# A fused gated-attention and ReGLU kernel: step 1's loads in another order and behind other events, and all engines' orders planned anew

## Chip, core and metric

The kernel runs on one core of one Trainium2 chip. The metric is device time in microseconds for one execution. Before the change it is 193.26 us, the median of five runs (192.61 to 194.41).

A core has five engines with a queue of instructions each: PE (TensorE, matrix products), ACT (ScalarE), DVE (VectorE), POOL (GpSimd) and SP (SyncE, which only issues DMA transfers here). Each works through its own queue in order and waits on semaphores for the others. Sixteen DMA engines carry all transfers; every load of this kernel is spread over all of them and has landed when the last of the sixteen has done its part.

## What is computed

Shapes: 4 batches, 8 heads, 768 tokens, head size 48; so 3072 tokens of 384 features go into the feed-forward network, whose hidden size is 1536.

```python
f = 1.0 / (1.0 + np.exp(-f_logit))
for t in range(S):
    state = f[:, :, t, :, None] * state + np.einsum('bhd,bhe->bhde', k[:, :, t], v[:, :, t])
    y[:, :, t] = np.einsum('bhd,bhde->bhe', q[:, :, t], state)
...
x = y.transpose(0, 2, 1, 3).reshape(B * S, H * D)
gate = np.maximum(x @ w_gate, 0.0)
val = x @ w_val
return (gate * val @ w_out).astype(np.float32)
```

## The kernel before

**Steps and pairs.** The 768 tokens are cut into six steps of 128 (steps 0 to 5, `c` in the code). Each step handles four blocks of 128 tokens, in two pairs of two; "f1.0" is the load of `f_logit` for step 1, pair 0. In steps 0 and 1 (`twos`) a pair is two consecutive 128-token chunks of one batch and goes through `attention_pair`; in steps 2 to 5 it is one chunk of each of two batches and goes through `attention_front` and `attention`.

**A pair's chain.** ACT turns f into log decays (L585, L586: exponential, then logarithm, into `bneg`). PE sums them along the tokens (L594). ACT takes exponentials (L608, `expo`), and k and q are multiplied by them into `hats` (L610): on POOL or on DVE, by the set `on_dve` and, in step 0, by a rule of its own. PE transposes `hats` (L642), k's first and q's second, DVE copies the result (L650, `qkT`), PE forms the scores (L667), DVE masks them (L683; two of them go by ACT and POOL, L678 and L680, set `by_pool`), and PE makes the rows (L712, L717), which ACT copies to `xT` (L729). POOL casts v into `vpad` (L657). The state goes by L692, L564, L568 and L570.

**The feed-forward part.** For each step `ffn_hidden` makes the hidden values, 12 blocks `j` of 128: PE multiplies `xT` by `wg` and by `wv` (L922), ACT takes the ReLU (L928), DVE the product (L932, `gT`). `ffn_out` multiplies by `wo` (L965), ACT copies (L975), SP stores (L979). PE fills the times between attention pieces with this work.

**Loads.** f, k, q and v come by SP, 384 KB each (L487). The weights come by POOL's queue, three slices of each of `wg`, `wv` and `wo` (L508); they are cast from f32 to bf16 on the way. The list `first` fixes the order of the loads of steps 0 and 1 and of all weight slices; "wg0@f0.1" means that POOL issues slice 0 of `wg` only once f0.1 has landed. Loads of SP are a chain among themselves, and so are those of POOL, and what an engine has queued behind such a wait waits too. Loads of steps 2 to 5 wait for the load three places ahead of them (`flight`).

**The planner.** The order in which each engine does its operations is worked out when the program is built. `Plan.schedule` is a list scheduler with a cost for each operation: at each step it takes the operation that can start first, by priority where several can. `Plan.transfers` simulates the two queues of loads packet by packet and gives each load of `first` a landing time, and `settle` goes through scheduling and transfers eight times. `tail` is the time that is assumed between a load's last packet and its landing, for POOL's loads and for SP's after 14 us. None of these numbers is executed; they set orders alone.

**Fillers.** Up to 15 us PE has gaps, in which products of a tile of zeros (`zeros`) keep it busy: 18 of 512 columns, one that is planned (L1015) and 17 put in gaps (L1024).

Of the kernel before, what the change touches and what calls it, by code (L numbers as in the profile page):

```python
# [8 lines left out]
BF16 = mybir.dt.bfloat16  # L9
# [33 lines left out]
class Plan:  # L43
# [143 lines left out]
    def transfers(self):  # L187

        rings = {e: [op for op in self.order[e] if op.parts] for e in ("SP", "POOL")}
        todo, at = {e: [] for e in rings}, {e: 0 for e in rings}  # L190
        issue = {"SP": 0.0}
        held = {e: [] for e in rings}
        sent, owed, t, last = 0, 0, 0.0, None
        pending = None
        sp = rings["SP"]
        queue = {e: [] for e in rings}
        for op in rings["POOL"]:
            queue["POOL"].append([op, op.parts[0], op.start + op.parts[3]])
# [24 lines left out]
        while True:  # L223
            feed()
            heads = {e: queue[e][0] for e in queue if queue[e]}
            if not heads:
                break
            can = {e: h for e, h in heads.items() if h[2] <= t}
            if not can:
                times = [h[2] for h in heads.values()]  # L230
                if nxt < len(sp) and pending is None:
                    times.append(max(sp[nxt].ready, issue["SP"]))
                t = max(t + 0.01, min(times))
                continue
            e = next(iter(can)) if len(can) == 1 else ("POOL" if last == "SP" else "SP")
            h = can[e]
            t += h[0].parts[1 if len(can) == 1 else 2] / 1000.0
            last = e
            h[1] -= 1
            if e == "SP":  # L240
                sent += 1
            if h[1] == 0:
                h[0].land = t + (self.tail[0] if e == "POOL" else 0.65 if t < 14.0 else self.tail[1])
                queue[e].pop(0)

    def settle(self, banks, rounds, early):
        self.depth, self.lag, self.tail = 250, 2.4, (1.6, 2.6)
        for i in range(rounds):
            self.schedule(banks)
            if i < rounds - 1:  # L250
                self.transfers()
                for op in self.ops:
                    if op not in early:
                        op.land = op.issued = None
        return self.order
# [47 lines left out]
def bass_hgrn2_outer__then__ffn_reglu_kernel(  # L303
# [14 lines left out]
    x_way = {(c, pr): "tiled" if c < 5 else "xbar" for c in range(6) for pr in range(2)}  # L318
    s_twin = {(c, pr) for c in range(6) for pr in range(2)}
    y_twin = {(c, pr) for c in range(2, 5) for pr in range(2)}  # L320
    on_dve = {(1, 0, 0, 0), (1, 0, 0, 1), (1, 1, 0, 0), (1, 1, 0, 1)}
    act_copies, dve_q, single = set(), set(), set()
    flight = 3
    wsteps = 3
    first = ("f0.0 k0.0 q0.0 v0.0 f0.1 k0.1 v0.1 wg0@f0.1 wv0 wg1 wv1 q0.1 wg2@wv0 wv2 f1.0@wv1 k1.0 q1.0 v1.0 wo0@q1.0 wo1 "
             "k1.1 f1.1 q1.1 v1.1@f1.1 wo2").split()
    B, H, S, D = q.shape
    C = 128
    NC = S // C
# [11 lines left out]
    sb = nc.alloc_sbuf_tensor  # L341
# [40 lines left out]
    mask2 = sb("mask2", [128, 2, 2, 64], BF16)  # L382
    ident = sb("ident", [128, 128], BF16)
    ones = sb("ones", [128, 1], BF16)
    zeros = sb("zeros", [128, 512], BF16)
    banks = [nc.alloc_psum_tensor(f"ps{i}", [128, 512], F32) for i in range(8)]

    pl = Plan({"bc": 2, "bc4": 4, "tp": 2, "s": 4, "y": 2, "kv": 2, "f": 4})
    add = pl.add
    gp, ve, sc, te, sy = nc.gpsimd, nc.vector, nc.scalar, nc.tensor, nc.sync  # L390
# [13 lines left out]
    def pool_t(n):  # L404
        return dict(occ=0.1 + n * 2.2 / 1000.0, lat=0.12)
# [29 lines left out]
    for t, name, src, sname in ((upto, "upto", tri, "tri"), (below, "below", tris, "tris")):  # L435
        add("DVE", lambda t=t, src=src: ve.tensor_tensor(t[:], src[:], same.ap[:, 0:128], ALU.mult), [same, sname], [name],
            occ=0.25, prio=-19)
    add("DVE", lambda: ve.tensor_copy(pick2[:], same.ap[:, 0:128].rearrange("p (b t) -> p b t", b=2)[:, :, 0]), [same], ["pick2"],
        occ=0.1, prio=-19)
    for i, src, name in ((0, upto, "upto"), (1, below, "below"), (1, upto, "upto")):  # L440
# [3 lines left out]
            src[:, 64:128].unsqueeze(1).to_broadcast([128, len(lo), 64]), ALU.add), [name], [f"mask2_{i}{m}" for m in lo],  # L444
            prio=-9, **pool_t(64 * len(lo)))

    fill("DVE", "zeros", zeros[:], 0.0, 256, -30)
    for i in range(NB):
        fill("DVE", f"bneg{i}", bneg[:, i], 0.0, 512, -28 if i < 1 else 11 if i < 2 else 30)
    for i in range(NH):  # L450
# [558 lines left out]
    for item in pend[:-1]:  # L1009
        ffn_out(*item)  # L1010
    ffn_end(NC - 1, B - 1, [(0, 256), (256, DM)])

    WARM = 512
    warm_until = 15.0
    add("PE", lambda: te.matmul(banks[-1][:, 0:WARM], zeros[:, 0:128], zeros[:, 0:WARM]), ["zeros"], ["warm"], occ=0.2,  # L1015
        prio=-30)
    for e in pl.ENGINES:
        pl.free0[e] = 0.8
    spare = banks[-1]
    order = pl.settle([(bk, warm_until if bk is spare else 0.0) for bk in banks], rounds=8, early=set(firsts))  # L1020
    waits = pl.needs()

    def warm():
        return te.matmul(spare[:, 0:WARM], zeros[:, 0:128], zeros[:, 0:WARM], start=True, stop=True, skip_group_check=True)  # L1024

    busy, at, begun = [], pl.free0["PE"], False
    for op in order["PE"]:
        gap, each = op.start - at, 0.44 if at < 4.0 else 0.23
        if begun and op.start <= warm_until:
            for _ in range(int((0.9 if gap > 1.5 else 0.6) * gap / each)):  # L1030
                busy.append((op, warm))
        begun = True
        at = op.start + op.occ
    fillers = {}
    for op, emit in busy:
# [2 lines left out]
    for e in ("PE", "ACT", "DVE", "POOL"):  # L1038
        n = 0
# [75 lines left out]
```

## Time and profile before

| what | value |
|---|---|
| median of five runs | 193.26 us |
| the profiled execution, its time | 193.03 us |
| its span, first to last instruction | 191.3 us |
| PE busy | 181.2 us, 95% of the span |
| DVE, ACT, POOL busy | 106.4, 109.7, 75.5 us |
| DMA moved | 32.04 MB, mean 167 GB/s |
| granted TensorE clock | 1.00 |

The first table below gives busy time by stretch; the DMA share is the mean over the 16 engines (queues overlap, so that it can pass 1).

| stretch, us | PE busy, us | DVE | ACT | POOL | DMA share |
|---|---|---|---|---|---|
| 0 to 16 | 12.90 of 16.00 | 13.41 | 10.18 | 12.77 | 0.99 |
| 16 to 45 | 25.39 of 29.00 | 21.50 | 16.11 | 12.46 | 1.13 |
| 45 to 100 | 54.74 of 55.00 | 33.42 | 39.39 | 30.35 | 1.15 |
| 100 to 150 | 49.37 of 50.00 | 26.37 | 29.30 | 19.88 | 0.83 |
| 150 to 191.3 | 38.82 of 41.30 | 11.70 | 14.74 | 0.00 | 0.14 |

The loads around the change, from the issues and landings that the trace gives:

| load | issued, us | to landing | landed |
|---|---|---|---|
| wg0, wv0, wg1 | 9.54, 10.47, 11.25 | 6.3, 7.3, 8.6 | 15.8, 17.8, 19.9 |
| wv1, wg2, wv2 | 15.01, 18.03, 19.95 | 6.7, 6.6, 6.8 | 21.7, 24.6, 26.8 |
| f1.0, k1.0 | 21.74, 22.15 | 7.4, 8.1 | 29.1, 30.3 |
| q1.0, v1.0 | 22.93, 26.70 | 8.5, 5.9 | 31.5, 32.6 |
| k1.1, f1.1 | 29.11, 30.27 | 5.3, 5.3 | 34.4, 35.6 |
| q1.1, v1.1 | 31.46, 35.58 | 12.2, 10.6 | 43.6, 46.2 |
| wo0, wo1, wo2 | 31.75, 32.55, 36.45 | 8.0, 10.1, 9.4 | 39.7, 42.6, 45.9 |
| f2.0 | 35.99 | 11.7 | 47.7 |

In the profile's lines an instruction group is given with its start, its length, engine, line and tiles; a bracket at the end gives the idle time of that engine just before it and what ended it. "issue" there means that the engine waited for nothing that the profile shows. A busy PE is one with a product in its pipeline; consecutive products overlap, so lengths of groups add up to more than the time they took.

### The profile page before, as it was taken

To read this page: it belongs to the slowest core of one execution; us is meant where nothing else is said; L and a number is where in the kernel's file an instruction comes from. 1 tells how busy PE (TensorE), PEld (TensorE's weight loads), DVE (VectorE), ACT (ScalarE), POOL (GpSimd) and SP (SyncE) were. 2 spreads that over 40 slices of the span, in tenths; PEclk is the share of its full clock that TensorE was granted. 3 is DMA by queue.
4 is the path that set the end of the run, shared out by engine and by line. 5 is a ranking of instruction groups with operands and counts; after the bars stand their busy time and mean duration, and the time that the engine had idled before them with its cause. 6 is when DMAs were issued, how large, how long until landed. Compare 5 with 4: busy or idle time off the path is not lost.

```text
span 191.3 us, 5012 instructions
## 1 busy us (share of the span) xinstructions
PE 181.2 (95%) x2061; PEld 107.9 (56%) x2079; DVE 106.4 (56%) x189; ACT 109.7 (57%) x244; POOL 75.5 (39%) x109
## 2 busy tenths in 40 slices
PE   7878899789999999999999999999999999999995
PEld 2456674446686456767645564554555555544564
DVE  7799365995736765617685284635528323343300
ACT  3785459734598576584877829566533533334322
POOL 8497503743295646547365563725400000000000
DMA  5999999999999999999999998999631310011113
GB/s 154 324 261 201 159 267 225 203 218 186 246 184 223 220 174 220 238 193 250 167 225 182 191 229 175 221 210 225 150 77 41 86 41 17 24 45 41 41 51 114
DMA packets 108854, 32.04 MB, mean 167 GB/s; under 512 B 101792, under 2 KB 108832, under 8 KB 108832
## 3 DMA queue, kind: packets, MB, share of 16 engines
q1 hardware_dynamic: 104848, 28.19, 70.6%
q0 software_dynamic: 3984, 3.54, 12.1%
q8 instruction: 16, 0.26, 0.5%
q14 instruction: 6, 0.05, 0.1%
HBM read 25.95 MB, written 4.72 MB: 160 GB/s over the span
## 4 chain that ended last, share of the span: by engine, by line
PE 76%; DMA 16%; POOL 4%; issue 2%; SPq 1%; ACT 0%; POOLq 0%
PE ps L922 41%; PE ps L965 23%; DMA q_in<-in_q_dram 7%; DMA wo<-in_moe_w_out_dram 5%; DMA wv<-in_moe_w_val_dram 4%; PE ps L852 3%; PE ps L817 2%; PE ps L751 1%; PE ps L900 1%; SPq L487 1%; PE ps L945 1%; POOL hats L610 1%; POOL vpad L657 1%; POOL wg L508 1%; PE ps L712 1%
## 5 line engine op out<-in xcount | busy, mean ns | idle before, releaser
L932 DVE TENSOR_TENSOR gT<-relu,ps 128x512 bf16<-128x512 bf16 (+1 forms) x88 | 51.1, 588 | 61.0 <-PE ps L922 37.6
L928 ACT ACTIVATE relu<-ps 128x512 bf16<-128x512 f32 (+1 forms) x88 | 45.5, 521 | 28.6 <-PE ps L922 27.3
L922 PE MATMUL ps<-xT,wv 128*128 128x512 bf16 (+1 forms) x262 | 60.7, 340 | 0.8 <-DMA wv<-in_moe_w_val_dram 0.5
L922 PE MATMUL ps<-xT,wg 128*128 128x512 bf16 (+1 forms) x249 | 57.9, 338 | 0.8 <-issue 0.2
L965 PE MATMUL ps<-wo,gT 128*128 128x384 bf16 x276 | 49.1, 326 | 0.3 <-DMA wo<-in_moe_w_out_dram 0.3
L965 PEld LDWEIGHTS ps<-wo,gT 128*128 128x128 bf16 x276 | 26.2, 98 | 18.5 <-DMA wo<-in_moe_w_out_dram 0.7
L922 PEld LDWEIGHTS ps<-xT,wv 128*128 128x128 bf16 x264 | 25.0, 98 | 19.7 <-DMA wv<-in_moe_w_val_dram 0.7
L922 PEld LDWEIGHTS ps<-xT,wg 128*128 128x128 bf16 x264 | 24.7, 98 | 19.6 <-issue 1.3
L975 ACT ACTIVATE osb<-ps 128x384 f32<-128x384 f32 x23 | 11.2, 494 | 25.8 <-PE ps L965 25.8
L827 DVE TENSOR_TENSOR ptm<-ps,tri 128x512 bf16<-128x512 f32 x32 | 20.5, 684 | 5.3 <-PE ps L817 5.2
L773 POOL TENSOR_TENSOR hats<-k_in,expo 128x384 bf16<-128x384 f32 x16 | 15.8, 998 | 18.1 <-ACT expo L761 15.2
L570 POOL TENSOR_TENSOR st<-ssum,dec 128x384 bf16<-128x384 f32 x16 | 13.1, 831 | 19.4 <-DVE ssum L568 19.3
L777 POOL TENSOR_TENSOR hats<-q_in,expo 128x384 bf16<-128x384 f32 x16 | 15.7, 997 | 5.2 <-DMA q_in<-in_q_dram 5.1
L568 DVE TENSOR_TENSOR ssum<-ps,st 128x384 f32<-128x384 f32 x16 | 8.4, 552 | 3.7 <-PE ps L900 3.5
L761 ACT ACTIVATE expo<-ps 128x384 f32<-128x384 f32 x16 | 7.9, 491 | 2.8 <-PE ps L754 2.7
L683 DVE TENSOR_TENSOR ptm<-ps,mask 128x512 bf16<-128x512 f32 x14 | 8.7, 681 | 1.1 <-PE ps L667 1.0
L807 POOL CAST vpad<-v_in 128x384 bf16<-128x384 f32 x16 | 7.6, 507 | 1.1 <-DMA v_in<-in_v_dram 1.1
L763 ACT ACTIVATE expo<-ps 128x384 f32<-128x384 f32 x16 | 8.0, 500 | 0.0
L729 ACT ACTIVATE xT<-ps 128x384 bf16<-128x384 f32 x8 | 4.2, 598 | 5.5 <-PE ps L717 5.5
L742 ACT ACTIVATE f_in<-f_in 128x768 f32<-128x768 f32 x8 | 6.7, 843 | 0.8 <-DMA f_in<-in_f_logit_dram 0.8
L744 ACT ACTIVATE bneg<-f_in 128x768 bf16<-128x768 f32 x8 | 6.7, 843 | 0.1
L881 ACT ACTIVATE xT<-ps 128x384 bf16<-128x384 f32 x12 | 5.2, 486 | 2.5 <-PE ps L852 2.5
(85 smaller groups left out, 162.2 us busy)
## 6 DMA issues: line engine op xcount, KB each, us to landing
f_in<-in_f_logit_dram SPq DMA_DIRECT2D x12, 384.0 KB, 5.8
k_in<-in_k_dram SPq DMA_DIRECT2D x12, 384.0 KB, 5.5
q_in<-in_q_dram SPq DMA_DIRECT2D x12, 384.0 KB, 4.8
v_in<-in_v_dram SPq DMA_DIRECT2D x12, 384.0 KB, 5.5
out_dram<-osb SPq DMA_DIRECT2D x23, 192.0 KB, 2.6
wg<-in_moe_w_gate_dram POOLq DMA_DIRECT2D x3, 384.0 KB, 6.6
wv<-in_moe_w_val_dram POOLq DMA_DIRECT2D x3, 384.0 KB, 6.8
wo<-in_moe_w_out_dram POOLq DMA_DIRECT2D x3, 384.0 KB, 9.4
```

Source lines behind the costliest of these rows:

```text
L568: add("DVE", lambda: ve.tensor_tensor(tmp[:, :], kv.ap[:, 0:HD], s_old[:, :], ALU.add), [kv, f"S{b}_{(c + 1) % 2}"], [key], prio=P + 8, ** ...
L570: add("POOL", lambda: gp.tensor_tensor(t4(s_new), t4(tmp), rate, ALU.mult), [key] + dk, [f"S{b}_{c % 2}"], prio=P + 8, **pool_t(HD))
L683: add("DVE", lambda i=i, j=j, mask=mask: ve.tensor_tensor(ptm[ms[i]][:, j, :, :], s[i][j].ap[:, :].rearrange("p (n t) -> p n t", n=NP), ma ...
L763: add("ACT", lambda: sc.activation(ex[:, 0, :], bc.ap[:, 0:HD], AF.Exp, scale=-1.0), [bc], [f"expq{ei // 2 * 2}_{ei % 2}"], prio=P + 1, ** ...
L773: add("POOL", lambda: gp.tensor_tensor(hk, kin[:, b % 2, :, :], ex[:, 1, :].rearrange("p (h d) -> p h d", h=H), ALU.mult), in_keys("k", c, ...
L777: add(e, lambda: engine[e].tensor_tensor(hq, qin[:, b % 2, :, :], ex[:, 0, :].rearrange("p (h d) -> p h d", h=H), ALU.mult), in_keys("q", ...
L827: add("DVE", lambda mi=mi, j=j, s=s: ve.tensor_tensor(ptm[mi][:, j, :, :], s.ap[:, :].rearrange("p (n t) -> p n t", n=NP), mask, ALU.mult) ...
L922: mm = te.matmul(bank.ap[:, 0:n], wt[:, kt, j * 128:(j + 1) * 128], xT[xi][:, kt, n0:n1], start=(kt == 0), stop=(kt == NK - 1))
L928: add("ACT", lambda: sc.activation(relu[ri][:, 0:n], gate.ap[:, 0:n], AF.Relu), [gate], [f"relu{ri}"], prio=P, **act_t(n))
L932: add("DVE", lambda: ve.tensor_tensor(gT[gi][:, j, n0:n1], relu[ri][:, 0:n], val.ap[:, 0:n], ALU.mult), [val, f"relu{ri}"], [f"gT{gi}_{j}_ ...
L965: mm = te.matmul(o[b].ap[:, 0:DM], gT[gi][:, j, b * C:(b + 1) * C], wo[:, j, :], start=(j == 0), stop=(j == NJ - 1))
L975: add("ACT", lambda b=b, oi=oi: sc.activation(osb[oi][:, :], o[b].ap[:, 0:DM], AF.Copy), [o[b]], [f"osb{oi}"], prio=P, **act_t(DM))
```

## The change

- In `first`, the order on SP after step 0 goes from f1.0 k1.0 q1.0 v1.0 k1.1 f1.1 q1.1 v1.1 to f1.0 k1.0 v1.0 k1.1 f1.1 q1.0 q1.1 v1.1, and in step 0 wg0's place in the list moves. The events behind which loads are released change: f0.1 and k0.1 get f0.0, v1.0 gets wv2, q1.0 gets f1.0, v1.1 has wo0 in place of f1.1; of the weights wg2 has k0.1 in place of wv0, wo0 has k1.1 in place of q1.0, and wo2 gets f1.1.
- In the planner, `transfers` takes a list of seven times (`fetch`) at each of which its simulated queues stand still for 0.55 us (`stall`); `tail` goes from 1.6 and 2.6 us to 1.0 and 0.7.
- One more k product, that of step 1, pair 1, first of its two halves, goes from POOL to DVE (`on_dve`).
- `zeros` has 128 columns in place of 512. The planned first filler has 128 columns; the others read the tile several times over (a broadcast) and stand in the first five gaps of PE's order that are planned longer than 0.4 us: 4 of 256 columns, then 8, 3, 1 and 2 of 512.
- With all this, the orders of all engines are worked out anew, those of the later steps too.

```diff
@@ transfers
+        fetch = list(self.fetch)
...
+            if fetch and fetch[0] <= t:
+                fetch.pop(0)
+                t += self.stall
+                last = None
+                continue
             e = next(iter(can)) if len(can) == 1 else ("POOL" if last == "SP" else "SP")
...
@@ settle
-        self.depth, self.lag, self.tail = 250, 2.4, (1.6, 2.6)
+        self.depth, self.lag, self.tail = 250, 2.4, (1.0, 0.7)
+        self.stall = 0.55
+        self.fetch = [14.1, 19.8, 26.3, 40.8, 45.8, 51.4, 57.8]
...
-    on_dve = {(1, 0, 0, 0), (1, 0, 0, 1), (1, 1, 0, 0), (1, 1, 0, 1)}
+    on_dve = {(1, 0, 0, 0), (1, 0, 0, 1), (1, 1, 1, 0), (1, 1, 0, 0), (1, 1, 0, 1)}
...
-    first = ("f0.0 k0.0 q0.0 v0.0 f0.1 k0.1 v0.1 wg0@f0.1 wv0 wg1 wv1 q0.1 wg2@wv0 wv2 f1.0@wv1 k1.0 q1.0 v1.0 wo0@q1.0 wo1 "
-             "k1.1 f1.1 q1.1 v1.1@f1.1 wo2").split()
+    first = ("f0.0 k0.0 q0.0 v0.0 f0.1@f0.0 wg0@f0.1 k0.1@f0.0 v0.1 wv0 q0.1 wg1 wv1 wg2@k0.1 f1.0@wv1 wv2 k1.0 v1.0@wv2 k1.1 f1.1 "
+             "q1.0@f1.0 q1.1 wo0@k1.1 wo1 wo2@f1.1 v1.1@wo0").split()
...
-    zeros = sb("zeros", [128, 512], BF16)
+    zeros = sb("zeros", [128, 128], BF16)
...
-    fill("DVE", "zeros", zeros[:], 0.0, 256, -30)
+    fill("DVE", "zeros", zeros[:], 0.0, 64, -30)
...
-    add("PE", lambda: te.matmul(banks[-1][:, 0:WARM], zeros[:, 0:128], zeros[:, 0:WARM]), ["zeros"], ["warm"], occ=0.2,
-        prio=-30)
+    add("PE", lambda: te.matmul(banks[-1][:, 0:128], zeros[:, :], zeros[:, :]), ["zeros"], ["warm"], occ=0.1, prio=-30)
...
-    def warm():
-        return te.matmul(spare[:, 0:WARM], zeros[:, 0:128], zeros[:, 0:WARM], start=True, stop=True, skip_group_check=True)
-
-    busy, at, begun = [], pl.free0["PE"], False
+    def warm(n):
+        return te.matmul(spare[:, 0:n * 128], zeros[:, :], zeros[:, :].unsqueeze(1).to_broadcast([128, n, 128]), start=True, stop=True,
+                         skip_group_check=True)
+
+    busy, at, wide = [], None, [(2, 4), (4, 8), (4, 3), (4, 1), (4, 2)]
     for op in order["PE"]:
-        gap, each = op.start - at, 0.44 if at < 4.0 else 0.23
-        if begun and op.start <= warm_until:
-            for _ in range(int((0.9 if gap > 1.5 else 0.6) * gap / each)):
-                busy.append((op, warm))
-        begun = True
+        gap = op.start - at if at is not None else 0.0
+        if wide and gap > 0.4:
+            n, many = wide.pop(0)
+            busy += [(op, lambda n=n: warm(n))] * many
         at = op.start + op.occ
```

More of the change, by code (lines that the diff above doesn't have):

```diff
@@ L1011, in bass_hgrn2_outer__then__ffn_reglu_kernel @@
     ffn_end(NC - 1, B - 1, [(0, 256), (256, DM)])
-    WARM = 512
-    warm_until = 15.0
-    add("PE", lambda: te.matmul(banks[-1][:, 0:WARM], zeros[:, 0:128], zeros[:, 0:WARM]), ["zeros"], ["warm"], occ=0.2,
-        prio=-30)
+    add("PE", lambda: te.matmul(banks[-1][:, 0:128], zeros[:, :], zeros[:, :]), ["zeros"], ["warm"], occ=0.1, prio=-30)
     for e in pl.ENGINES:
@@ L1019, in bass_hgrn2_outer__then__ffn_reglu_kernel @@
     spare = banks[-1]
-    order = pl.settle([(bk, warm_until if bk is spare else 0.0) for bk in banks], rounds=8, early=set(firsts))
+    order = pl.settle([(bk, 15.0 if bk is spare else 0.0) for bk in banks], rounds=8, early=set(firsts))
     waits = pl.needs()
-    def warm():
-        return te.matmul(spare[:, 0:WARM], zeros[:, 0:128], zeros[:, 0:WARM], start=True, stop=True, skip_group_check=True)
-    busy, at, begun = [], pl.free0["PE"], False
+    def warm(n):
+        return te.matmul(spare[:, 0:n * 128], zeros[:, :], zeros[:, :].unsqueeze(1).to_broadcast([128, n, 128]), start=True, stop=True,
+                         skip_group_check=True)
+    busy, at, wide = [], None, [(2, 4), (4, 8), (4, 3), (4, 1), (4, 2)]
     for op in order["PE"]:
-        gap, each = op.start - at, 0.44 if at < 4.0 else 0.23
-        if begun and op.start <= warm_until:
-            for _ in range(int((0.9 if gap > 1.5 else 0.6) * gap / each)):
-                busy.append((op, warm))
-        begun = True
+        gap = op.start - at if at is not None else 0.0
+        if wide and gap > 0.4:
+            n, many = wide.pop(0)
+            busy += [(op, lambda n=n: warm(n))] * many
         at = op.start + op.occ
```

## The prediction

> **What bounds the kernel now.** I began with the busy row of TensorE (PE) by slices, to see where PE is not full.
>
> ```profile
> PE   7878899789999999999999999999999999999995
> ```
>
> Each digit is 4.78 us. From the tenth slice on (43 us) every digit but the last is 9: PE is the bound there. So the end of the kernel is PE's work plus PE's idle time, and only idle time can be won. Next, who PE waited for, first from 5 to 45 us, then from 45 us to the end.
>
> ```profile
> PE ps L667 <- DVE qkT L650: 1.3, 3, 0.6
> PE ps L642 <- DVE hats L610: 1.1, 2, 0.8
> PE ps L717 <- issue: 0.9, 1, 0.9
> PE ps L712 <- POOL ptm L680: 0.6, 1, 0.6
> PE ps L922 <- DMA wv<-in_moe_w_val_dram: 0.5, 1, 0.5
> ...
> PE ps L965 <- DMA wo<-in_moe_w_out_dram: 0.3, 1, 0.3
> ...
> PE ps L922 <- issue: 0.2, 1, 0.2
> ```
>
> The columns are total us, times, longest. The lines shown make 4.7 us before 45 us (left out: 0.4 for the first gates, 0.2 of "issue"), and 0.2 us (the last line, the only one of the second answer) after it. A new order can win at most the former and can only lose in the latter. Now the chain that ended last, up to where PE takes it over, and the places in time where PE stood.
>
> ```profile
> 15.01 6.71 DMA wv<-in_moe_w_val_dram
> ...
> 22.93 8.53 DMA q_in<-in_q_dram
> ...
> 31.75 0.43 POOL wo L508
> ...
> 32.55 10.06 DMA wo<-in_moe_w_out_dram
> ```
> ```profile
> 36.97 0.62 PE L642 MATMUL ps<-ident,hats 128*128 128x128 bf16 x8 [0.84 <-DVE hats L610]
> ...
> 38.19 0.59 PE L922 MATMUL ps<-xT,wv 128*128 128x512 bf16 x2 [0.16 <-issue]
> 39.36 0.64 PE L667 MATMUL ps<-qkT 48*64 48x128 bf16 x32 [0.57 <-DVE qkT L650]
> ...
> 42.65 1.48 PE L965 MATMUL ps<-wo,gT 128*128 128x384 bf16 x8 [0.29 <-DMA wo<-in_moe_w_out_dram]
> ```
>
> The chain (start, length) says: wv1 lands, releases step 1's loads; q1.0 lands, releases wo; wo1 lands at 42.6, and PE takes over. But PE had other work meanwhile, so this chain is not worth its length. What the stretch of 36 to 43 us costs is the four brackets: 0.84 + 0.16 + 0.57 + 0.29 = 1.86 us. The first has this behind it (DVE, POOL, and DVE again one pair later):
>
> ```profile
> 32.86 4.05 DVE L610 TENSOR_TENSOR hats<-q_in,expo 128x384 bf16<-128x384 f32 x2 [0.41 <-ACT expo L608]
> 33.31 1.96 POOL L610 TENSOR_TENSOR hats<-k_in,expo 128x384 bf16<-128x384 f32 x2
> ...
> 43.71 1.03 DVE L610 TENSOR_TENSOR hats<-q_in,expo 128x384 bf16<-128x384 f32 x2 [0.49 <-DMA q_in<-in_q_dram]
> ```
>
> The same two products took 4.05 us while POOL was running its own, and 1.03 us when POOL was quiet.
>
> **Step 0: nothing.** f0.1 and k0.1 now wait on SP for f0.0, with every later load queued behind. f0.0 was issued at 0.81 and landed 3.4 later, 4.2; f0.1 left at 4.25 before. The wait is covered; at most 0.1 us. The zeros memset (0.27 us for 256 elements) shrinks to about a quarter; DVE has time there. Fillers: 18 of 512 columns become 1 of 128, 4 of 256 and 14 of 512. A cold 512 took 3.17/7 = 0.45 us. Four of 256 are 0.9 us inside the gap to 2.22; eight of 512 are 3.6 us from 2.44, ending at 6.0, just when the prefix sums (L594) became ready at 6.03; at worst 0.3 us late. Three instead of six before L642 leave PE idle for about 0.8 us; it idled 1.3 us at 21 us and the next 256-column products still came 0.11 us apart. I take 0, bounds 0 and +0.3.
>
> **Weights of gate and val.** POOL stood 1.35 us for wv0 before it issued wg2 at 18.03. With wg2 behind k0.1 (5.60 + 4.8 = 10.4) that wait goes. wg0, wv0, wg1, wv1 landed at 15.8, 17.8, 19.9 and 21.7, about 1.95 us apart; wg2 and wv2 can follow at 23.7 and 25.6, where they came at 24.6 and 26.8. No PE wait hangs on them, so directly 0. They share the engines with f1.0 and k1.0, though, which should land 1.1 us earlier: 28.0 and 29.2 (before 29.1 and 30.3). PE's 0.5 us for wv0 stays: wv0 is second on its queue as before.
>
> **Step 1's loads.** SP now stops before v1.0 until wv2 has landed (25.6), with k1.1, f1.1, q1.0 and q1.1 queued behind it. A load on quiet engines took 3.4 us to land; v1.0 on full ones took 5.9. I take the middle, 30.2 (bounds 29.0 and 31.5). Loads then followed each other at 1.15 to 1.2 us (SP's spacing in step 0) or 1.33 (step 1 before); with 1.27: k1.1 31.5, f1.1 32.7, q1.0 34.0, q1.1 35.3. So q1.0 comes 2.5 us later than before (31.5), and q1.1 8 us earlier (it was issued at 31.46 and landed 12.2 later, among the wo slices). The later q1.0 is no loss: POOL's k products need only k1.0 and should be done by about 34, so the q products run without POOL beside them, 1.03 us, to 35.1 instead of 36.9. L642 for q starts at 35.2 instead of 36.97, the scores (L667) after one copy (0.65) and half a microsecond of transposes at 36.8 instead of 39.36. The 0.84, 0.16 and 0.57 go: **-1.57**. Break-even is q1.0 at 36.97 - 1.03 = 35.9.
>
> **Output weights.** wo0 waits on POOL for k1.1 (31.5; it was issued at 31.75). Behind it in POOL's order may stand the k products; a POOL blocked until 31.5 still starts them before the old 33.31. wo0 landed 8.0 us after issue in a crowd, wg0 after 6.3: 38.7 taken, 37.9 to 39.6. wo1 1.95 later, 40.7 (was 42.6); wo2, behind f1.1, 42.6 (was 45.9). PE wants wo0 at 40.89 - 1.57 = 39.3 and wo1 1.3 later, 40.6. The 0.29 becomes 0.1: **-0.19** (bounds -0.29 and +0.4). v1.1 waits on SP for wo0, with step 2's loads and the first stores behind; f2.0 had been used at 47.8 and now is issued at 39 and needs about 6: covered.
>
> **One k product of pair (1,1) on DVE.** 1.0 us leaves POOL, 0.55 us joins DVE. PE is in the output product then: 0.
> The Trainium skill (SBUF — State Buffer, "SBUF: two separate sides") speaks against it: VectorE and GpSimd share one port pair by an exclusive lock, and the later one stands still for the whole instruction. By it this DVE product and POOL's other k product run one after the other, 1.0 + 0.55 us instead of side by side; by the rows, 4.05 against 1.03, they do hinder each other, but behind cover, so either way the sum keeps its 0.
>
> **PE's own stop.** One matmul of L717 at 22.14 stood 0.95 us for nothing the profile shows. I take it to be PE's instruction supply: the page shows 16 instruction packets of 0.26 MB in all, 16 KB each. The change has as many PE instructions, so I leave it: 0, bounds -0.95 (gone) and +0.5 (a second).
> The skill's Runtime: NRT & Kernel Launch ("Instruction fetch mechanics") calls the crossing of a 16 KiB block mostly hidden; by it the stop would be something else and could vanish, making the sum 0.95 us lower. No run here shows which.
>
> **All later orders.** The planner's new constants change only simulated times, but every order after 45 us is planned again. Before, PE waited 0.2 us there: nothing to win. I take +0.2, bounds 0 and +1.5 (one wait of the size of the stops above).
>
> **Sum:** -1.57 - 0.19 + 0.2 = -1.56 on the profiled execution's 193.03 us (span 191.3): 191.5. The median of the five runs, 193.26, lies 0.23 higher: **191.7 us**.
>
> **Rivals.** (a) *The waits close* as above, 190.9 to 192.5: chance 0.50. (b) *The wait moves to wo*: PE reaches the output product earlier than wo lands, because wo0 is released no earlier than before. If wo0 keeps 39.7 and wo1 41.7, PE, ready at 39.3, waits 0.4 + 0.7 instead of 0.29, and with +0.5 later only about 0.3 us remain: 193.0; for it speaks that wo's release moves from 31.75 to only 31.5; against it that q1.1 and v1.1 no longer crowd it. 0.23. (c) *More goes*: PE's stop too, and PE's 0.5 us for wv0 or the 0.6 us for POOL's mask product, since POOL no longer stands 1.35 us: -1.56 - 0.95 - 0.4 gives 190.3. 0.10. (d) *Slower: q1.0 falls among the wo slices*, as q1.1 did, whose 12.2 us against f1.1's 5.3 are 6.9 us of crowding. wo0 is issued at 31.5 and weights need some 4 us before they take engines; q1.0 must be out by then. If not, and 60% of 6.9 us hits it, it lands at 38.1, its transposes start at 39.2 instead of 36.97, PE stands 2.2 us more than before and regains 0.9 elsewhere: 194.6. It decides once q1.0 lands after 35.9. For it: three loads now stand ahead of q1.0 behind a new SP wait; against it: two loads' time of margin. 0.17.
>
> What this kernel's measurement tells from no change is 0.5%, 1.0 us. Faster by more takes (c) and most of (a), whose upper end 192.5 is within it: 0.57. Within 0.5%: (b) and the rest of (a): 0.27. Slower: 0.16 of (d). The range goes from just below (c) to part of (d): 189.9 to 194.2.
>
> **What would show it.** Right: q1.0 landing between 33 and 35.5, q products of pair (1,0) near 1.0 us for two, no bracket over 0.3 us on L642 and L667 near 35 to 38 us, wo1 landed before 41.5, first full FFN group of step 1 (53.78 before) near 52. Wrong: a PE bracket on hats or wo above 0.8 us there, any PE wait over 0.5 us after 45 us, or a POOL that stands for k1.1 with the k products behind it.

## The result

The changed kernel takes 192.91 us (median of 44 runs, 191.97 to 194.54). The kernel before, run beside it 79 times, takes 192.14 us (191.37 to 195.29). The ratio is 1.0043, with a 95% interval of 1.0029 to 1.0057: the change makes the kernel slower by 0.4%, where 0.8% faster was forecast. The median of before is 1.1 us lower than that of the five runs shown above, from which the forecast of 191.7 us was counted down.

The changed kernel's profiled execution took 193.33 us (span 191.6), that of before 193.03 (191.3). Lines of code after `transfers` have numbers higher by 8: L642 of before is L650 now, L667 is L675, L712 is L720, L965 is L973. The busy row of TensorE by slices, from the page of the changed kernel:

```profile
PE   7887799989999999999999998999999999999995
```

The 8th slice (33.5 to 38.3 us) has gone from 7 to 9, where the stops were that the forecast wanted to close. The 9th (38.3 to 43.1 us) is at 8 still, the 4th and the 5th (14 to 24 us) are at 7 where they were 8, and the 25th (115 to 120 us) is a new 8. Who PE waited for between 5 and 45 us in the changed kernel (total us, times, longest):

```profile
PE ps L650 <- DVE hats L618: 1.1, 2, 0.8
PE ps L725 <- issue: 1.0, 1, 1.0
PE ps L675 <- DVE qkT L658: 0.8, 1, 0.8
PE ps L720 <- POOL ptm L688: 0.4, 1, 0.4
PE ps L930 <- DMA wv<-in_moe_w_val_dram: 0.3, 1, 0.3
...
PE ps L720 <- DVE ptm L691: 0.3, 1, 0.3
```

The waits for wo are gone, as forecast. So are those for q's hats and for the scores of pair (1,0): the 0.8 us on hats is step 0's, at 8 us, and the 0.8 us on qkT is step 0's too, at 17 us; the rest of the hats row and the last row are new. PE's pieces at 38 to 43 us in the changed kernel show what is new:

```profile
38.31 0.64 PE L675 MATMUL ps<-qkT 48*64 48x128 bf16 x32
...
40.38 0.62 PE L650 MATMUL ps<-ident,hats 128*128 128x128 bf16 x8 [0.23 <-DVE hats L618]
40.98 1.47 PE L973 MATMUL ps<-wo,gT 128*128 128x384 bf16 x8
42.77 0.74 PE L720 MATMUL ps<-ptm,vpad 64*32 64x128 bf16 x64 [0.32 <-DVE ptm L691]
```

DVE in the same stretch, changed kernel:

```profile
35.43 1.02 DVE L618 TENSOR_TENSOR hats<-q_in,expo 128x384 bf16<-128x384 f32 x2
...
38.03 0.55 DVE L618 TENSOR_TENSOR hats<-k_in,expo 128x384 bf16<-128x384 f32 x1
38.49 1.82 DVE L618 TENSOR_TENSOR hats<-q_in,expo 128x384 bf16<-128x384 f32 x2
40.24 2.47 DVE L691 TENSOR_TENSOR ptm<-ps,mask 128x512 bf16<-128x512 f32 x4
```

The two q products of pair (1,0) take 1.02 us, as forecast. But DVE now has three products of pair (1,1), the first of them the k product that the change gave it, ahead of the masks of pair (1,0), whose scores PE made at 38.31. PE runs into both: it stands 0.23 us for the last product and 0.32 us for the masks. The chain that ended last in the changed kernel runs through just these two pieces of DVE and from there to PE's rows (L720) at 42.77:

```profile
38.11 2.21 DVE hats L618 x3
40.32 2.40 DVE ptm L691 x4
```

A second loss lies late in the kernel. PE and ACT in the changed kernel, where step 5 begins:

```profile
115.54 0.84 ACT L750 ACTIVATE f_in<-f_in 128x768 f32<-128x768 f32 x1 [1.61 <-DMA f_in<-in_f_logit_dram]
...
118.41 0.50 PE L759 MATMUL ps<-bneg,tri 128*128 128x384 bf16 x2 [0.61 <-ACT bneg L752]
```

ACT stands 1.61 us for f5.0 with two copies of `xT` queued behind it, and PE stands next.

**The two executions compared.** To see where two kernels part, I took from each trace the time at which PE had done equal amounts of product work (each product at its usual duration, fillers left out), which is good to about 0.1 us. Set against the profiled execution of before, the changed kernel gained 1.33 us by the scores of pair (1,0), at 39 us; lost 0.58 from there to 54 us and 1.06 after that, 0.79 of it at 118 us: +0.31, the difference of the two times (193.33 - 193.03). So on those two executions the forecast gain is there, and was given back. The next section shows that the gain is measured against stops which further traces of before don't have.

### The profile page after: what moved, and what is told of

It is laid out like the page before. It is cut to its first block, busy times and chain, and to the rows that moved or that the text cites. A ratio compares the mean times of both kernels' runs of the same rounds, so it can differ in the third digit from the quotient of the medians.

```text
span 191.6 us, 5013 instructions
## 1 busy us (share of the span) xinstructions
PE 181.6 (95%) x2062; PEld 107.9 (56%) x2080; DVE 104.2 (54%) x190; ACT 109.6 (57%) x244; POOL 74.2 (39%) x108
## 4 chain that ended last, share of the span: by engine, by line
PE 75%; DMA 9%; ACT 5%; DVE 4%; issue 2%; POOL 1%; SPq 1%; POOLq 0%; DVEq 0%
PE ps L930 42%; PE ps L973 22%; DMA wv<-in_moe_w_val_dram 4%; DMA f_in<-in_f_logit_dram 3%; DMA q_in<-in_q_dram 2%; PE ps L860 2%; PE ps L825 2%; DVE hats L618 2%; PE ps L759 1%; ACT relu L936 1%; DVE ptm L691 1%; PE ps L720 1%; PE ps L908 1%; PE ps L953 1%; DVE gT L940 1%
## 5 line engine op out<-in xcount | busy, mean ns | idle before, releaser
L930 PE MATMUL ps<-xT,wv 128*128 128x512 bf16 (+1 forms) x258 | 59.8, 339 | 0.8 <-DMA wv<-in_moe_w_val_dram 0.3
L930 PE MATMUL ps<-xT,wg 128*128 128x512 bf16 (+1 forms) x252 | 58.7, 339 | 1.0 <-issue 0.5
L973 PE MATMUL ps<-wo,gT 128*128 128x384 bf16 x276 | 49.5, 326 | 0.0
L973 PEld LDWEIGHTS ps<-wo,gT 128*128 128x128 bf16 x276 | 26.1, 98 | 18.1 <-DVE ptm L691 0.3
L815 POOL CAST vpad<-v_in 128x384 bf16<-128x384 f32 x16 | 7.7, 506 | 0.6 <-DMA v_in<-in_v_dram 0.6
L665 POOL CAST vpad<-v_in 128x384 bf16<-128x384 f32 x8 | 3.9, 506 | 9.1 <-DMA v_in<-in_v_dram 9.1
```

Source lines behind the costliest of these rows:

```text
L930: mm = te.matmul(bank.ap[:, 0:n], wt[:, kt, j * 128:(j + 1) * 128], xT[xi][:, kt, n0:n1], start=(kt == 0), stop=(kt == NK - 1))
L973: mm = te.matmul(o[b].ap[:, 0:DM], gT[gi][:, j, b * C:(b + 1) * C], wo[:, j, :], start=(j == 0), stop=(j == NJ - 1))
```

## The experiments

Two more traces of each kernel came first: b1 and b2 are the kernel before, a1 and a2 the changed kernel, unedited.

> Edit: none, the kernel before, for a second trace of it. Theory F (its first trace was a slow execution, 193.03 against a median of 192.14 over 79 runs, and the stops of 0.84 and 0.57 us near 37 us are longer there than usual): those two stops together under 1.0 us, PE 0.5 to 1 us earlier at 50 us than in the first trace. Rival G (the first trace is typical in that stretch, and the execution lost its 0.9 us elsewhere): the two stops stay within 0.2 us of 1.4 together. Ratio 1.000.

> Edit: none, the changed kernel, for a second trace of it. Theory A: the wait of 0.6 us on step 5's f at 118 us is there again. Theory H (that wait belongs to single executions, as the trace of the kernel with one k product put back on POOL, with the same PE, ACT and SP orders, has none of it): no PE wait over 0.3 us after 60 us; then the change's 0.43% must stand before 60 us. Ratio 1.003 to 1.006.

> Edit: none, the kernel before, a third trace. As for the second: theory F, stops at 37 and 39 us together under 1.0 us; rival G, 1.2 to 1.6 us.

> Edit: none, the changed kernel, a third trace. Theory A: the wait at 118 us again, about 0.6 us; theory H: none over 0.3 us after 60 us, and what sets it behind the kernel before lies between 5 and 60 us.

Before: 192.15 against 191.97 us, ratio 1.0004 [0.9974, 1.0034]; changed: 192.89, 1.0050 [1.0021, 1.0080]; single times 191.85 (b2) and 192.77 (a2). Theory F held: the two stops are gone from both further traces of before. So did theory H: neither a1 nor a2 has a PE wait over 0.3 us after 60 us (what a2 loses there, in the table below, lies in shorter ones). The same stretch in b1, POOL and DVE, then PE:

```profile
32.86 2.27 POOL L610 TENSOR_TENSOR hats<-k_in,expo 128x384 bf16<-128x384 f32 x2 [1.16 <-ACT expo L608]
33.19 2.35 DVE L610 TENSOR_TENSOR hats<-q_in,expo 128x384 bf16<-128x384 f32 x2 [0.47 <-ACT expo L608]
35.85 1.06 PE L642 MATMUL ps<-ident,hats 128*128 128x128 bf16 x16
...
38.04 0.64 PE L667 MATMUL ps<-qkT 48*64 48x128 bf16 x32
...
39.52 2.77 PE L965 MATMUL ps<-wo,gT 128*128 128x384 bf16 x16
```

No bracket on PE's lines: the 0.84, 0.57 and 0.29 us on which the forecast stood aren't there. q1.0 landed at 29.9 us here and at 30.5 in b2, against 31.5 in the first trace (one DMA engine finished 1.9 us after the median engine there, 1.0 in b1, 1.7 in b2). POOL therefore issued wo at 30.16 (31.75 in the first trace) and was through with it before its k products could start; DVE's q products took 2.35 us, not 4.05.

A late q1.0 alone doesn't make these stops. In s45, a run described further down that is the kernel before with other fillers, q1.0 landed at 31.4 us and POOL issued wo at 31.72 and began its k products at 33.29, all as in the first trace; but DVE began after POOL, not before it (POOL, then DVE):

```profile
33.29 2.27 POOL L610 TENSOR_TENSOR hats<-k_in,expo 128x384 bf16<-128x384 f32 x2
33.62 2.35 DVE L610 TENSOR_TENSOR hats<-q_in,expo 128x384 bf16<-128x384 f32 x2 [0.47 <-ACT expo L608]
```

PE has no stop on hats or scores there. All seven traces in which POOL begins 0.33 us before DVE (b1, b2, s45, s90, y_qearly, y_qearly2, y_best) have 2.35 us, or 2.36, and no such stop; of the traces with before's orders the first is the only one in which DVE begins first.

What each stretch cost, as delays against b1 (same method; the rows further down are of the experiments that follow):

| trace | up to 22.6 us | 22.6 to 39.4 | 39.4 to 54 | 54 to end | sum |
|---|---|---|---|---|---|
| before, first | -0.33 | +1.65 | +0.04 | 0 | +1.36 |
| b2 | -0.31 | 0 | +0.48 | 0 | +0.17 |
| changed, first | +0.09 | -0.10 | +0.62 | +1.06 | +1.67 |
| a1 | -0.03 | -0.09 | +0.62 | -0.01 | +0.49 |
| a2 | -0.23 | -0.09 | +0.95 | +0.47 | +1.10 |
| y_frozen | -0.17 | +1.37 | -0.43 | 0 | +0.77 |
| y_frozen2 | -0.35 | +1.08 | -0.42 | +0.97 | +1.28 |
| y_qearly | -0.20 | 0 | -0.46 | +1.60 | +0.94 |
| y_qearly2 | +0.89 | 0 | -0.48 | 0 | +0.41 |
| y_best | -0.22 | 0 | -0.46 | 0 | -0.68 |

The times in the head are b1's. The first stretch holds the start of the kernel and PE's own stop near 21 us, and varies by itself. The change is worth 0.1 us at 22.6 to 39.4 us where 1.57 was forecast, and costs 0.6 us or more at 39 to 54 us in each of its three traces. (In a2 0.33 of the 0.95 lie inside the group of rows at 42.45 us, 1.07 us long instead of 0.74.) The two together make 0.5 to 0.9 us, the size of the 0.77 us between the two medians.

**Taking back one piece of the new orders.** Five edits of the changed kernel:

```diff
@@ x_act, after settle: two copies of xT ahead of step 5's decay on ACT
...
+    seq = copies + decay + mid
+    acts[lo:hi + 1] = seq
...
@@ x_pool: the extra k product goes back to POOL
-    on_dve = {(1, 0, 0, 0), (1, 0, 0, 1), (1, 1, 1, 0), (1, 1, 0, 0), (1, 1, 0, 1)}
+    on_dve = {(1, 0, 0, 0), (1, 0, 0, 1), (1, 1, 0, 0), (1, 1, 0, 1)}
@@ x_pe, after settle: the second 8 output products ahead of the rows of pair (1,0)
...
+    pe[at:at + 3] = rest + [rows]
...
@@ x_fill: other fillers
-    wide = [(2, 4), (4, 8), (4, 3), (4, 1), (4, 2)]
+    wide = [(4, 1), (4, 7), (4, 6), (4, 1), (4, 2)]
@@ x_all: x_act, x_pool and x_pe together
```

> Edit: in the changed kernel's ACT order alone, the two xT copies of step 4's first pair are moved ahead of step 5's f exponential and logarithm (prio 200), and the logarithm follows the exponential at once. Theory A (the front of the change wins 0.7 us, and ACT's order gives it back at 117 us, because ACT stands 1.6 us for f5.0 with ready copies behind it): PE's 0.6 us wait on L759's input is gone, PE is 0.5 to 0.8 us earlier from 118 us to the end, ratio to before 0.999 to 1.001 where the change gave 1.0043. Rival B (the load stream itself sets PE's pace in steps 4 and 5, whatever the order): PE stops by as much at another load within 10 us, ratio stays at 1.003 to 1.005.

> Edit: the k product of step 1, pair 1, first half, goes back from DVE to POOL; nothing else, PE's, ACT's and SP's orders are the same. Prediction's step (it lies behind cover): no difference to the change within 0.001, 1.003 to 1.005 against before. Rival: the products of pair (1,1) collide on DVE and POOL and the transposes after 39 us come up to 1 us later: ratio 1.006 to 1.009.

> Edit: in the changed kernel's PE order alone, the second eight output products of step 0's first pair (L973, on wo1) go ahead of the rows of step 1's first pair (L720, L725). Theory I (the change's loss lies between 39 and 54 us: DVE makes the products of pair (1,1) before it masks the scores of pair (1,0), and PE, with too little output work planned in between, stands 0.33 us for hats and 0.42 us for the masks): the 0.42 is gone, PE about 0.4 us earlier at 54 us, ratio 1.001 to 1.003 where the change has 1.0043. Rival A (the loss is the wait on step 5's f): ratio stays 1.004 to 1.005.

> Edit: the changed kernel with the old number of fillers: 1, 7, 6, 1 and 2 of 512 columns in the five gaps instead of 4 of 256 and 8, 3, 1, 2 of 512; orders as in the changed kernel. Theory C (PE's late start of 0.4 us by 22 us comes from the fillers: the first sums at 6.1 us ran with 0.29 to 0.32 us per 384-column product instead of 0.17): with the old fillers they are 0.17 apart again and PE is 0.2 to 0.4 us earlier at 22 us, ratio 1.002 to 1.003. Rival D (when PE turns fast differs from execution to execution and the fillers don't matter): ratio the same as the change's within 0.001.

> Edit: three edits on the changed kernel: the k product back on POOL, PE's order as in the run before this one, ACT's order of step 5's f as in the first experiment. Theory I with A: all three stops (0.33, 0.42, and the occasional one at 118 us) are gone, ratio 0.998 to 1.001. Rival J (something else that no PE stop shows makes up most of the 0.43%): 1.002 to 1.004.

| kernel | ratio to before | interval |
|---|---|---|
| changed | 1.0043 | 1.0029 to 1.0057 |
| x_act | 1.0034 | 1.0011 to 1.0056 |
| x_pool | 1.0041 | 1.0017 to 1.0065 |
| x_pe | 1.0049 | 1.0008 to 1.0091 |
| x_fill | 1.0032 | 1.0002 to 1.0062 |
| x_all | 1.0024 | 0.9985 to 1.0063 |

None differs from the changed kernel by what can be told, and no ratio came down to what the theories expected that looked for the loss in these stops (A for x_act, I for x_pe, I with A for x_all), though the intervals of x_pe and x_all don't exclude it. The stops do move. In x_pool the wait on hats is gone and that for the masks is longer; in x_pe the wait for the masks is gone and a longer one comes at the next scores (one line of each trace, PE):

```profile
42.51 0.73 PE L720 MATMUL ps<-ptm,vpad 64*32 64x128 bf16 x64 [0.44 <-DVE ptm L691]
```
```profile
45.19 0.64 PE L675 MATMUL ps<-qkT 48*64 48x128 bf16 x32 [0.71 <-ACT xT L737]
```

In x_pe the rows come later by the products put ahead of them, and the wait at 45 us is for ACT's copy of those rows. In x_all the stops on hats, on masks and at 118 us are absent, but 0.70 us at those scores and 0.80 us at 107 us, on f4.1, are there instead. With x_act the stop at 118 us was absent from its one trace, but so it was in a1 and x_pool, which have the change's order there; the median didn't fall by enough to tell.

**Fillers.** x_fill was to show whether the change's fillers leave PE at a slow pace at the start. Two more kernels with other fillers, s90 and s45, were built for PE's own stop near 21 us (last section) and bear on this too. In the kernel before, 7 and 6 fillers of 512 columns were replaced by 72 and 30 small ones and 2 and 2 large ones (s90), or by 36 and 16 and 4 and 4 (s45):

```diff
...
+        few, keep = plan.get(len(had), (0, len(had)))
+        fillers[op] = [lambda i=i: tiny(i) for i in range(few)] + had[:keep]
```

> Edit: the kernel before, its fillers changed: in the two largest gaps 72 and 30 small products (32 columns of weights, 32 columns) and 2 and 2 of 512 columns stand in place of 7 and 6 of 512; 93 products more. Theory K (PE's stop of 1.0 to 1.7 us near 21 us comes after the same number of PE instructions in all ten traces so far, 347 weight loads and 346 products, so it is PE's supply of instructions): it now falls after the same count, 93 products earlier in the program, near 17 us, partly inside waits that PE has there anyway; L717's chain runs through; PE 0 to 1.2 us earlier at 30 us; ratio 0.994 to 1.000. Rival L (it hangs on L717's place, on what these products read): it stays in L717; ratio 1.000 to 1.003.

> Edit: the same with 36 and 16 small products and 4 and 4 of 512: 47 products more. Theory K: the stop after 347 weight loads and 346 products again, so 47 products earlier in the program than before, in L712's chain near 20 us; length as it takes to the same arrival, 1 to 2 us; ratio 0.998 to 1.002. Rival L: in L717, ratio 1.000 to 1.002.

s90 1.0042 [0.9998, 1.0086], s45 1.0040 [1.0001, 1.0078]. The 72 small products take far less time than the five large ones they stand for, so that PE stood 1.85 us at the first prefix sums (s90, PE):

```profile
2.44 0.77 PE L1040 MATMUL ps<-zeros 128*32 128x32 bf16 x72
...
6.02 0.50 PE L594 MATMUL ps<-bneg,upto 128*128 128x384 bf16 x1 [1.85 <-ACT bneg L586]
6.32 0.53 PE L594 MATMUL ps<-bneg,below 128*128 128x384 bf16 x1
```

The sums start 0.30 us apart, PE's slow pace; in the first trace of before they were 0.17 apart. But b1, a1 and the changed kernel's first trace have 0.29 or 0.30 there as well, and b2 and a2 0.17: it differs between executions of one kernel. With before's fillers or x_fill's 2 of 10 traces have the slow pace, with the change's 5 of 8; among the three traces each of before and of the changed kernel, the slow ones are 0.2 to 0.3 us later at 22.6 us. Whether the change's fillers make the slow pace more frequent is open; x_fill's ratio, 1.0032, can't be told from 1.0043.

**Loads or orders?** Four kernels separate the two. x_oldloads is the changed kernel with the old list `first`, x_newloads the kernel before with the new list; both are planned anew. y_frozen (and y_frozen2, the same again) is the kernel before with the new list put in after planning, so that PE, ACT, DVE and POOL keep before's orders.

```diff
@@ y_frozen, after settle; now is the change's list
+    for op in firsts:
+        op.deps = {d: how for d, how in op.deps.items() if d not in firsts}
...
+    for item in now:
+        item, _, behind = item.partition("@")
+        turn.append(done[item])
+        if behind:
+            done[item].deps[done[behind]] = "raw"
...
```

> Edit: the changed kernel with the old list of loads and releases, all orders planned anew with the new constants. Theory A: without the new loads the 1.1 us that PE gained between 35 and 41 us is gone (stops of 0.5 to 1 us on hats or qkT near 37 us, wo1 landing at 42 or later), ratio 1.004 to 1.012. Rival E (the new loads win nothing; what PE gained there came from the planner's constants): the gain stays, ratio 0.998 to 1.004.

> The kernel before with the change's load list, and all orders planned anew with before's own planner constants (tail 1.6 and 2.6 us, no fetch stops), before's fillers and on_dve. Theory O (a replanned order costs unless it happens to fit): ratio anywhere from 0.998 to 1.006, and what it costs is seen as stops of PE at 30 to 54 us on hats, masks or scores, not on wo or wv. Theory G (the loads gain and only the change's own constants spoil it): 0.993 to 0.997. Theory L (the loads cost): 1.003 or more with the stops where a load lands.

> The kernel before with the change's load list alone: the same loads in the new order on SP and behind the new events, while PE, ACT, DVE and POOL keep before's orders and before's fillers. It leaves out the new planner constants, the extra k product on DVE, and the new fillers. Theory O (the loads do no harm, and the loss of some 0.6 us at 39 to 54 us comes from the orders that were planned anew): ratio to before 0.997 to 1.001, wo landed by 41 us, no stops of PE on hats or masks between 39 and 43 us over 0.15 us. Theory L (the new loads themselves cost, for example q1.0 that now lands at 33.4 in place of 29.9 to 31.5): ratio 1.003 to 1.006, with a stop of PE on hats of pair (1,0) near 36 us of 0.5 us or more. Theory G (the loads' gain is real and the new orders give it back): 0.993 to 0.996.

> The kernel of y_frozen again (before's orders and fillers, with the change's load list), to narrow its 1.0017 [0.9993, 1.0042]. Theory Q (under before's orders q1.0, which lands at 34 us in place of 30, makes DVE begin its q products 1.1 us late and stops PE by some 1.3 us at 36 to 39 us, of which part comes back because wo is there earlier): ratio 1.001 to 1.004, with the stops at L642 and L667 again. Rival (the stops of y_frozen's trace are of that one execution): no stop over 0.3 us there, ratio 0.998 to 1.000.

x_oldloads 1.0067 [1.0042, 1.0091]; x_newloads 1.0107 [1.0079, 1.0135]; y_frozen 1.0017 [0.9993, 1.0042]; y_frozen2 1.0031 [0.9992, 1.0069]. Planned anew with the change's constants, the old list is no better than the new one (1.0043). The ratio of x_oldloads is the one that theory A gave, but its one trace doesn't have A's stops near 37 us (0.31 us on scores, wo1 landed at 41.3). In x_newloads, above the range of theory O, the waits are spread: before 45 us 1.4 us on scores, 0.9 on hats made by POOL and 0.4 on masks, and 0.70 us at 103.81 us, some 60 us after the last load that was moved. Between x_newloads and the two y_frozen runs, which have the same loads, lie 0.8%: that is what planning anew can cost by itself. In y_frozen nothing but loads has moved, and theory O's "no stops" failed there. DVE, then PE:

```profile
34.33 2.45 DVE L610 TENSOR_TENSOR hats<-q_in,expo 128x384 bf16<-128x384 f32 x2 [1.78 <-DMA q_in<-in_q_dram]
...
36.84 0.62 PE L642 MATMUL ps<-ident,hats 128*128 128x128 bf16 x8 [0.56 <-DVE hats L610]
...
39.23 0.64 PE L667 MATMUL ps<-qkT 48*64 48x128 bf16 x32 [0.57 <-DVE qkT L650]
```

These are the forecast's stops, made by the change's own list: q1.0 lands at 34.2 us (33.7 in y_frozen2), DVE is free at 32.5, and PE loses 1.1 to 1.4 us by 39.4. So theory L holds for this one load, though the ratio fell between the theories. On the other side the list gains 0.43 us against b1 from there to 54 us. About half of it comes since wo2 lands at 42.6 us instead of 44.5 (in b1 PE's next output products begin at 44.54, just behind that landing); the other half lies inside the rows (L712), 0.97 us long in b1 and 0.73 in y_frozen, and no run shows that the loads make it, as the three traces of before have 0.73, 0.97 and 0.82.

**q1.0 back in its place.** If the late q1.0 is what costs, then the rest of the list should gain. y_qearly is y_frozen with two entries put back; y_qearly2 is the same again; y_best also puts load f5.0 ahead of a store on SP.

```diff
@@ y_qearly, the list now
-           ... wg2@k0.1 f1.0@wv1 wv2 k1.0 v1.0@wv2 k1.1 f1.1 q1.0@f1.0 q1.1 wo0@k1.1 wo1 wo2@f1.1 v1.1@wo0
+           ... wg2@k0.1 f1.0@wv1 wv2 k1.0 q1.0 v1.0@wv2 k1.1 f1.1 q1.1 wo0@q1.0 wo1 wo2@f1.1 v1.1@wo0
@@ y_best, SP's order
...
+    sp[at - 1:at + 1] = [f5, sp[at - 1]]
```

> As y_frozen, but with q1.0 back in its place right behind k1.0 and ahead of the load that waits for wv2, and with wo0 behind q1.0 as before. Theory Q: q1.0 lands near 30 us, DVE's q products begin at 33.2 or earlier, the stops at 36 to 39 us go, and the ratio is 0.3 to 0.7% below that of y_frozen2, 0.995 to 1.000. Rival (the loads have nothing to do with it): the same ratio as y_frozen2 within 0.2%.

> The kernel of y_qearly again (before's orders, the change's load list with q1.0 third as before). If its 0.9959 [0.9922, 0.9996] holds: ratio 0.994 to 0.999. If it was luck of that chip: 0.999 to 1.003. In the trace no stop on hats of pair (1,0), and perhaps the stop for step 5's f near 117 us, which costs 0 to 1.6 us.

> As y_qearly, with one more change: on SP the load f5.0 goes ahead of the store that stood before it and was waiting for ACT until 107.7 us. Theory C (what is won early is given back near 117 us because f5.0 is issued behind that store): f5.0 is issued 1 to 2 us earlier, the stop at L751 goes, and the ratio is 0.2 to 0.6% below that of y_qearly2. Rival (f5.0 lands late by one lagging DMA engine whenever it is issued): same ratio within 0.2%, and the stop stays in some traces.

y_qearly 0.9959 [0.9922, 0.9996], on one chip with y_frozen2's 1.0031; y_qearly2 0.9953 [0.9913, 0.9994]; y_best 0.9971 [0.9929, 1.0012]. In y_qearly q1.0 lands at 29.8 and wo2 at 42.5 us. DVE and PE:

```profile
32.99 2.35 DVE L610 TENSOR_TENSOR hats<-q_in,expo 128x384 bf16<-128x384 f32 x2 [0.47 <-ACT expo L608]
...
35.65 1.06 PE L642 MATMUL ps<-ident,hats 128*128 128x128 bf16 x16
...
37.84 0.64 PE L667 MATMUL ps<-qkT 48*64 48x128 bf16 x32
```

No stop is left there, and by 54 us it is 0.66 us ahead of b1. Theory Q held: 0.7% lie between y_frozen2 and y_qearly, and the stops of 1.1 to 1.4 us are gone. Two entries differ, q1.0's place and wo0's release; the stops themselves were on q1.0's products. This version is faster than the kernel before in both of its measurements, by about 0.45%, with intervals that just leave out no change; beside the changed kernel it wasn't measured.

y_qearly's trace still loses 1.60 us later on. The expectations of the last two runs place that at 117 us; its rows are these, twelve microseconds earlier (ACT and PE):

```profile
103.31 0.84 ACT L742 ACTIVATE f_in<-f_in 128x768 f32<-128x768 f32 x1 [2.16 <-DMA f_in<-in_f_logit_dram]
...
105.42 0.34 PE L751 MATMUL ps<-bneg,tri 128*128 128x384 bf16 x1 [1.36 <-ACT bneg L744]
```

It is the same kind of wait as the changed kernel's at 118 us, for f4.1 here, where one DMA engine finished 2.2 us after the median engine; f5.0 there was 2.1 us behind. y_frozen2 has it as well (0.69 us at 105.77), y_qearly2 and y_best haven't. So such a wait comes with before's orders too, and no run shows that the change brings it.

y_best, then, moved a load that was not the late one. What it shows is only whether f5.0 comes earlier for being issued earlier: at 105.98 us in y_best, at 108.41 in y_qearly2. Issued 2.4 us earlier it took 7.2 us instead of 4.6 and landed at 113.2 against 113.0. So it fits the rival, in which the lagging engine sets the landing: the last engine finished 1.9 us after the median engine in y_best and 0.9 in y_qearly2, so that the median engine was 0.8 us earlier. It is one pair of executions, and the two ratios can't be told apart.

## Why the prediction failed

- **The term of -1.57 us** ("The 0.84, 0.16 and 0.57 go") is the step that failed. It took three brackets of one execution as the kernel's habit. Two further traces of the same kernel have none of them: POOL's k products begin 0.33 us before DVE's q products there, not 0.45 us after, and the whole 1.65 us go without any change; the change itself is worth 0.1 us there. y_frozen shows the other side: "the later q1.0 is no loss" is wrong under before's orders, with the break-even near 33 us, where DVE's q products begin in b1 and y_qearly, not at 35.9. The signs of being right were taken from the same trace: the changed kernel has q1.0 at 33.5 us, 1.02 us for the two q products, no bracket over 0.3 us on pair (1,0) and wo1 at 40.8, all as listed; only the full feed-forward group of step 1 begins at 53.03 instead of near 52, and b1 has it at 52.43.
- **The range:** 192.91 us lies within 189.9 to 194.2, but on the wrong side of before. The forecast counted from a median of 193.26 that later runs of the same kernel put at 192.14, so that the time came near by luck.
- **Output weights, -0.19:** the landing was right by luck. wo0 and wo1 landed at 38.8 and 40.8 us (forecast 38.7 and 40.7), wo2 at 44.0 (42.6). But POOL, which has its k products ahead of wo now, issued wo0 only at 33.96, not at 31.5, and it took 4.9 us to land, not 7.2; the two errors cancel. The wait for wo is gone, 0.29 in the first trace of before, 0.69 in b2, none in b1. Under before's orders the list gains 0.42 to 0.48 us against b1 at this place, about half of it by wo2; under the new orders no gain is seen.
- **The landing times:** f1.0 27.0 (28.0), wv2 25.8 (25.6), v1.0 29.4 (30.2), k1.1 31.2 (31.5), q1.0 33.5 (34.0), q1.1 34.7 (35.3). Rival (d) did not come: q1.0 landed before POOL issued wo. Its "some 4 us" before weights take engines isn't in the traces (in the first trace of before wg0 is issued at 9.54 us and POOL's queue has its first packets at 12.0). Apart from the luck with wo, the landings of step 1 were forecast within 1 us; when the loads were needed was not.
- **One k product on DVE, 0:** PE met it in 0.23 us of stop, since DVE had masks queued behind. The ratio of x_pool doesn't differ by what can be told (1.0041 and 1.0043), so the sum's 0 stands within about 0.3%.
- **All later orders, +0.2 (0 to +1.5):** mis-sized, and looked for too late. The three traces show +0.6 to +0.95 us at 39 to 54 us, a stretch that the prediction counted as won. The late waits for f lie within its bounds, but aren't shown to belong to the new orders.
- **Step 0, weights' queue: 0**, as far as the traces tell; POOL's 1.35 us for wv0 went, and wv2 came 1 us earlier than in the first trace of before, but no earlier than in b1 (25.75 us in both). **Fillers, 0 (0 to +0.3):** open within these bounds, as said above.
- **PE's own stop, 0:** it stayed, at 0.8 to 1.4 us, in the three traces of both kernels.

What stays open: the loss at 39 to 54 us was moved by single edits and never brought back, so which pair of operations in the new DVE and PE orders makes it isn't shown; and how often the late wait for f strikes each kernel, for which the traces are too few.

## What to carry to other kernels

A stop of half a microsecond in one trace is a candidate, not a habit: look whether it hangs on a race that another execution can decide otherwise (here DVE began 0.45 us before POOL, elsewhere 0.33 us after it), and take a second trace before pricing it. A load has slack only up to the moment at which its reader is free, which is read from the reader's own row and not from the stop it ends in. Change the list of loads with all orders held fixed first: here two such kernels, each measured twice, told which part of the list lost, where planning all orders anew hid the effect behind costs of up to 0.8% of its own.

## What the runs showed of the hardware

**PE stops once near 21 us, waiting for nothing that the profile shows, in 19 of the 20 traces.** In b1 and in s90 (PE):

```profile
22.48 0.22 PE L717 MATMUL ps<-qkT,st 128*32 128x128 bf16 x1 [1.42 <-issue]
```
```profile
20.93 0.39 PE L922 MATMUL ps<-xT,wg 128*128 128x256 bf16 x2 [1.67 <-issue]
```

It falls after 347 weight loads in all 19, also in s90, where 93 more products stand ahead of it and this count lies in another piece of the program, as theory K had it (the ratio didn't fall as K expected). In s45, with 47 more, K failed: nothing stops after 347 loads, and the one stop near there, 0.98 us at 23.39, is for wv1, which landed at 23.34. So s90 speaks for a stop that goes with the instruction stream and not with data, s45 leaves it unexplained, and what makes it isn't shown. The Trainium skill's Runtime: NRT & Kernel Launch ("Instruction fetch mechanics") calls the crossing of an instruction block mostly hidden; whether this stop is such a crossing no run shows. It costs 0.8 to 1.7 us, and PE goes on between 21.9 and 22.6 us in 16 of the 18 traces that keep either kernel's fillers or x_fill's. That would swallow time won before it, which no run here tests.

**DVE and POOL hinder each other by an amount that differs with who starts first:** the same two q products took 4.05 us (first trace of before, DVE 0.45 us ahead, the only such trace), 2.35 (b1, POOL 0.33 us ahead, and six more traces) and 1.02 (changed kernel, POOL quiet). The Trainium skill's SBUF — State Buffer ("SBUF: two separate sides") makes the shared port an exclusive lock for the whole instruction. By it the four products, two of about 1.0 us and two of 0.5, would take an estimated 3.0 us end to end in either case. b1 has 2.68 (32.86 to 35.54); the first trace of before has 4.05 (32.86 to 36.91), with DVE begun first and through last, and two casts of POOL (1.29 us from 35.21) in between. Neither is the estimate, and the measurement decides: in b1 the products overlapped by some 0.3 us, and in the first trace the engine that began first was through last. The two ends lie 1.4 us apart.

**A load issued 2.4 us earlier landed no earlier** (f5.0, 113.2 us in y_best against 113.0 in y_qearly2), in one pair of executions, of which y_best was 1.1 us ahead by then.
